# Another order of instructions, loads and PSUM banks in a fused attention and maxout-MoE kernel

## The chip, the cores and the metric

The kernel runs on one NeuronCore of a Trainium2 chip, in one launch. The metric is the device time of that core in microseconds (us). The profile of one execution gives the start and the duration of every instruction and of every DMA packet. Its engines are named as the profile names them: PE (TensorE matmul), PEld (its weight loads), ACT (ScalarE), DVE (VectorE), POOL (GpSimd) and SP (SyncE, which here only issues DMAs).

## The reference

Attention over 8 batches and 8 heads with 1152 keys of width 64; neighbouring query rows are averaged, so there are 576 queries. The result, as 4608 tokens of width 512, goes through a small MoE-like block, in which the larger of two projections is projected back.

```python
q_pool = q.reshape(B, H, S // 2, 2, D).mean(axis=3)
scores = np.matmul(q_pool, k.transpose(0, 1, 3, 2)) / np.sqrt(D)
attn = softmax(scores)
x = np.matmul(attn, v)          # then (B, H, S/2, D) -> (B*S/2, H*D) = (4608, 512)
g = np.maximum(x @ w1, x @ w2)  # w1, w2: 512 x 1024
out = g @ w_out                 # w_out: 1024 x 512
```

## The kernel before

The 64 heads are taken in 32 pairs; a pair's two heads lie in the two halves of the 128 partitions. The work of a pair goes through these steps.

- **Loads.** q, k and v of a pair, 576 KB each, come by DMAs that SP issues (`load_q` L358, `load_k` L346, `load_v` L370). The weights come in between (`w_load` L379).
- **Casts.** POOL turns them into bf16: `cast_k` L405, `cast_q` L435 (adds the two neighbouring query rows), `cast_v` L445. For the first pair small pieces are cast on ACT, POOL and DVE (`cast_k0` L418 and L424, `cast_q0` L428).
- **Transposes.** Scores need q and k with the head's width in the partitions. For pairs 0 to 4 PE transposes both (`qtrans` L533, `ktrans_pe` L552) and DVE copies the result from PSUM (L540, L568). For pairs 5 to 31 k is transposed by a DMA (`ktrans` L475, issued by SP) and q by eight DVE instructions (`qtrans_dve` L485).
- **Scores and exponentials.** Keys times queries of all pairs form one long row, which is cut into 324 groups of 512 columns for both heads. `scores` L302 (called S below) fills two PSUM banks on PE with 64-row matmuls, and `exps` L317 (E) takes the exponential on ACT. A group that crosses from an odd pair to the next is cut in two on ACT, which makes 336 instructions.
- **Values.** `av_jobs` (L621, and L636 for the last 64 queries of a pair) multiplies exponentials by values on PE with 128-row matmuls, 9 in a chunk; DVE divides by the sum (L651, L654). For some pairs POOL first copies the exponentials of the last 64 queries aside (`keep_rest` L468).
- **Transposed x.** A DMA transpose (`xtrans` L703, L712), or PE and DVE for some pairs (`xtrans_pe` L552, L730, L733, L738), brings x to xT.
- **MoE.** max(x w1, x w2) is computed as x w2 + max(x (w1 - w2), 0). POOL makes the difference of the weights (`w_diff` L506), DVE casts the rest (`w_cast` L498), PE multiplies w2 by w_out once (`w2t_job`, `w_job` L593). Then `h_jobs` (L760, 64-row matmuls) and `p_job` (L803) run over tokens; DVE or ACT empties their banks (L771/L775 and L809/L812), and SP stores the result (L829, L835). The last 256 tokens go through `z_job` (L846) and `store_z` (L866).

At the start PE also runs matmuls that nobody reads (`fill`, L515): 28 at once and 16 pairs of them, one after each letter F.

The order is written out by hand. One long string of letters is read from left to right, and each letter appends one operation to the list of its engine: S a score group, E an exponential, A a chunk of values, digits parts of the MoE jobs and the emptying of their banks, l a load, t a DMA transpose of k, x one of xT, o a store, k, q, v and d the casts and differences on POOL, r a DVE transpose, F a fill. Every engine runs its own list strictly in order, and an operation waits by semaphores for what it reads and for the buffers that it overwrites. So the string matters only by the order inside each engine, with one exception: a load also waits for an exponential, chosen by where its letter stands.

```python
K0_ENG = ('ACT', 'ACT', 'POOL', 'POOL')
PACE = 2
PACE_FROM = 40
...
        def pace():
            g = done[0] - PACE
            return [f"E{g}"] if PACE and g >= PACE_FROM else []
...
            elif c == "E":
                g, go = exp_at.pop(0)
                go()
                done[0] = g
```

`done` is the last exponential group that the string has named, so a load whose letter follows E of group 230 is issued no earlier than the end of group 228. The order of the loads stands in LOADS, the PSUM bank of each job in BANKS (one digit for each score group or job, in the order in which they are opened), the order of MoE jobs in MOE, and that of the weight casts and differences in W_CASTS and W_DIFFS. There are three buffers each for raw q, k and v and for the transposed q and k.

## Time and profile before

| | |
|---|---|
| time, median of 3 runs | 359.64 us (359.12 to 360.29) |
| the profiled execution's own time | 358.12 us |
| its span, first to last instruction | 356.4 us |
| PE busy | 346.0 us (97%) |
| ACT busy | 313.8 us (88%) |
| DVE busy | 230.1 us (65%) |
| POOL busy | 151.4 us (42%) |
| granted TensorE clock, mean | 0.999 |
| HBM read and written | 62.91 MB and 9.44 MB |

Busy time of PE is modelled at the ends of its matmuls, so overlapping matmuls read as one busy stretch. In a row of the chain of waits the columns are the start and the length in us and the work that held the end at that time. In a row of the timeline they are the start and the length in us, engine, line, operation, tiles, shape, count, and in brackets the idle time before it and what ended it. In a row of groups they are the busy us, the mean ns of one, and the idle us before. A row of stretches gives for each engine the busy us and the number of instructions, then the granted clock, the DMA engines' busy share and GB/s.

### The profile page before, as it was taken

Reading aid. Unit: us, or ns where it says so; the run is one execution under the profiler, and the core shown is the slowest. Engines: PE = TensorE matmul, PEld = TensorE weight load, DVE = VectorE, ACT = ScalarE, POOL = GpSimd, SP = SyncE. Lnnn points to the kernel's source line nnn. Section 1 sums busy time; section 2 is a strip of 40 time slices with the busy share of each in tenths; the row PEclk is TensorE's granted clock in tenths of the full one; section 3 lists DMA queues with packets and bytes.
Section 4 is the critical chain, followed back from the end, with each engine's and each line's share of the span. In section 5 each row is a group of like instructions: output and inputs, shape, how many; then the busy total and the mean of one; then the engine's idle time right before and its main releaser. Section 6 shows DMA issues by size and latency. Waiting matters only on the chain.

```text
span 356.4 us, 13757 instructions
## 1 busy us (share of the span) xinstructions
PE 346.0 (97%) x6178; PEld 218.5 (61%) x6178; DVE 230.1 (65%) x472; ACT 313.8 (88%) x354; POOL 151.4 (42%) x136
## 2 busy tenths in 40 slices
PE   7889999999899999999999999999999999999996
PEld 5556665656564675656666576556576757448753
DVE  2587589974966867985887677785586875414001
ACT  5999999999999899999999989989999796992431
POOL 2625997554564264355544455227444621010000
PEclk9999999999999999999999999999999999999999
DMA  8999999999989989998999699998999943012215
GB/s 271 403 397 398 370 255 309 280 289 261 293 252 279 315 196 350 237 301 183 278 320 260 153 230 301 237 314 234 224 299 255 267 68 75 17 32 47 61 31 148
DMA packets 76699, 84.55 MB, mean 237 GB/s; under 512 B 48480, under 2 KB 49760, under 8 KB 76640
## 3 DMA queue, kind: packets, MB, share of 16 engines
q1 hardware_dynamic: 75856, 83.15, 87.5%
q8 instruction: 48, 0.79, 0.9%
q10 hardware_dynamic: 784, 0.52, 0.5%
q14 instruction: 11, 0.09, 0.1%
HBM read 62.91 MB, written 9.44 MB: 203 GB/s over the span
## 4 chain that ended last, share of the span: by engine, by line
PE 87%; ACT 9%; DMA 2%; issue 1%; SPq 0%; DVE 0%
PE ps L803 25%; PE ps L621 20%; PE ps L302 19%; PE ps L760 16%; ACT et L317 9%; PE ps L636 3%; PE ps L593 2%; DMA qraw<-in_q_dram 2%; PE ps L846 1%; PE ps L552 0%; PE ps L533 0%; SPq L346 0%; DVE qp L428 0%; SPq L358 0%; PE ps L730 0%
## 5 line engine op out<-in xcount | busy, mean ns | idle before, releaser
L317 ACT ACTIVATE et<-ps 128x1024 bf16<-128x1024 f32 (+1 forms) x336 | 302.4, 1019 | 14.5 <-PE ps L302 9.7
L302 PE MATMUL ps<-qpT,kT 64*128 64x256 bf16 (+7 forms) x1162 | 117.3, 283 | 2.7 <-issue 1.1
L485 DVE STREAM_TRANSPOSE qpT<-qp 32x288 bf16<-32x288 bf16 x216 | 101.4, 469 | 10.4 <-PE ps L302 6.1
L760 PE MATMUL ps<-xT,wd 64*128 64x512 bf16 (+3 forms) x832 | 81.2, 311 | 0.2
L302 PEld LDWEIGHTS ps<-qpT,kT 64*128 64x128 bf16 x1162 | 48.3, 94 | 49.7 <-ACT et L317 11.3
L803 PE MATMUL ps<-wo,stage 64*128 64x512 bf16 x544 | 76.4, 376 | 0.0
L435 POOL TENSOR_TENSOR qp<-qraw 128x576 bf16<-128x576 f32 x30 | 42.1, 1406 | 61.1 <-DMA qraw<-in_q_dram 57.3
L621 PEld LDWEIGHTS ps<-vE,et 128*128 128x128 bf16 x1728 | 54.9, 97 | 13.9 <-ACT et L317 9.3
L621 PE MATMUL ps<-vE,et 128*128 128x65 bf16 x1728 | 60.7, 193 | 0.7 <-issue 0.3
L771 DVE TENSOR_SCALAR stage<-ps 128x1024 bf16<-128x1024 f32 (+3 forms) x41 | 39.7, 970 | 21.1 <-PE ps L760 20.6
L760 PEld LDWEIGHTS ps<-xT,wd 64*128 64x128 bf16 x832 | 35.6, 94 | 22.2 <-PE ps L760 1.9
L405 POOL TENSOR_SCALAR kbf<-kraw 128x1152 bf16<-128x1152 f32 x31 | 35.7, 1153 | 26.3 <-DMA kraw<-in_k_dram 25.6
L803 PE MATMUL ps<-w,xT 64*128 64x512 bf16 x272 | 40.8, 377 | 0.0
L803 PEld LDWEIGHTS ps<-wo,stage 64*128 64x128 bf16 x544 | 26.4, 94 | 20.5
L445 POOL TENSOR_SCALAR vE<-vraw 128x1152 bf16<-128x1152 f32 x24 | 27.4, 1154 | 19.4 <-PE ps L636 10.8
L809 DVE COPY stage<-ps 128x1024 f32<-128x1024 f32 x14 | 17.1, 1224 | 23.1 <-PE ps L803 23.0
L468 POOL TENSOR_SCALAR stage<-et 128x1152 bf16<-128x1152 bf16 x14 | 16.1, 1152 | 35.5 <-ACT et L317 35.5
L654 DVE TENSOR_TENSOR xnat<-ps,rc 128x256 bf16<-128x256 f32 (+2 forms) x71 | 27.6, 397 | 2.0
L651 DVE RECIPROCAL rc<-ps 128x4 f32<-128x4 f32 (+2 forms) x64 | 11.6, 182 | 25.9 <-PE ps L621 25.5
L621 PEld LDWEIGHTS ps<-stage,et 128*128 128x128 bf16 x576 | 18.1, 97 | 2.7 <-issue 2.6
L621 PE MATMUL ps<-stage,et 128*128 128x65 bf16 x576 | 19.7, 193 | 0.0
L803 PEld LDWEIGHTS ps<-w,xT 64*128 64x128 bf16 x272 | 12.5, 94 | 8.8 <-DVE stage L771 0.2
(55 smaller groups left out, 155.4 us busy)
## 6 DMA issues: line engine op xcount, KB each, us to landing
vraw<-in_v_dram SPq DMA_DIRECT2D x32, 576.0 KB, 6.1
kraw<-in_k_dram SPq DMA_DIRECT2D x31, 576.0 KB, 6.7
qraw<-in_q_dram SPq DMA_DIRECT2D x31, 576.0 KB, 6.3
out_dram<-stage SPq DMA_DIRECT2D x24, 256.0 KB, 4.1
out_dram<-stage SPq DMA_DIRECT2D x21, 128.0 KB, 3.4
xT<-in_moe_w_dram SPq DMA_DIRECT2D x4, 512.0 KB, 12.2
stage<-in_moe_w_out_dram SPq DMA_DIRECT2D x4, 512.0 KB, 14.1
stage<-in_moe_w_dram SPq DMA_DIRECT2D x4, 512.0 KB, 13.2
```

Of the source, the lines that this page charges most:

```text
L302: last = e.matmul(ps[:, h, col:col + hi - lo], kT[i % 3][rows(h), t, :], qpT[i % 3][rows(h), lo:hi], start=True, stop=True)
L317: op("ACT", lambda e: e.activation(et2[:, :, c:c + z - a], ps[:, :, a - g * W:z - g * W], EXP, scale=scale), r=[f"b{m}", f"b{m + 1}"], w=w ...
L405: op("POOL", lambda g: g.tensor_scalar(kbf[s][:, :, :, :].rearrange("p t h d -> p h t d"), kraw[r][:, :, :, :], 1.0, 1.0, ALU.mult, ALU.mu ...
L435: op("POOL", lambda g: g.tensor_tensor(qpf[s][:, :, :], qraw[r][:, :, 0, :], qraw[r][:, :, 1, :], ALU.add), r=[f"qraw{r}"], w=[f"qp{s}.0", ...
L445: return g.tensor_scalar(vE[r][:, :, :, 0:D].rearrange("p t h d -> p h t d"), vraw[s][:, :, :, :], 1.0, 1.0, ALU.mult, ALU.mult)
L485: op("DVE", lambda e: e.transpose(view[dst:dst + 32, :, 32 * pb:32 * pb + 32], qpf[s][src:src + 32, :, 32 * db:32 * db + 32]), r=[f"qp{s}. ...
L621: last = e.matmul(fb[m][:, at * 66:at * 66 + 65], et[:, a:a + P], vE[vs][:, t, half, 0:65], start=(t == 0), stop=(t == NT - 1))
L654: todo.append(evac_op("DVE", lambda e, m, z=z, at=at, num=num, dst=dst: e.tensor_tensor(dst, a(m)[z, at:at + num, 0:D], rc[k][z, at:at + n ...
L760: last = e.matmul(fb[m + k][:, 0:size], wd[z, ct, (f0 + k) * P:(f0 + k + 1) * P], xT[z, ct, n0:n1], start=(turn == 0 and ct == 0), stop=(t ...
L771: return e.tensor_scalar_max(gT[:, f0:f0 + 2, g0:g0 + size], wide[m // 2][:, :, 0:size], 0.0)
L803: last = e.matmul(fb[m + k][:, :], lhs, rhs, start=(turn == 0 and j == 0), stop=(turn == 1 and j == NC_ + NF - 1))
L809: return e.tensor_copy(osb2[:, o:o + 2, :], wide[m // 2][:, :, :])
```

## The change

No operation, shape, buffer or tile is added or removed, and no wait is added by hand: the waits follow from the order. What is written differently is the string of letters, LOADS, BANKS, MOE, W_CASTS and W_DIFFS. Only the beginnings of the long ones are shown.

```diff
-    W_CASTS = ((0, 1), (0, 3), (0, 0), (0, 2), (2, 0), (2, 1), (2, 2), (2, 3))
-    W_DIFFS = ((3, 0), (3, 1), (1, 0), (2, 0), (2, 1), (0, 0), (0, 1), (1, 1))
+    W_CASTS = ((0, 1), (0, 3), (0, 2), (0, 0), (2, 1), (2, 2), (2, 0), (2, 3))
+    W_DIFFS = ((3, 1), (3, 0), (1, 1), (0, 1), (0, 0), (2, 1), (1, 0), (2, 0))
...
-        ("k", 3), ("w", 0, 0), ("w", 0, 2), ("v", 1), ("w", 2, 0), ("w", 2, 1), ("w", 2, 2), ("q", 3),
-        ("w", 2, 3), ("w", 1, 3), ("v", 2), ("w", 1, 2), ("k", 4), ("w", 1, 1), ("q", 4), ("q", 5),
-        ("k", 5), ("v", 3), ("w", 1, 0), ("k", 6), ("q", 6), ("q", 7), ("k", 7), ("v", 4), ("v", 5),
+        ("k", 3), ("w", 0, 2), ("w", 0, 0), ("v", 1), ("w", 2, 2), ("w", 2, 1), ("w", 2, 0), ("q", 3),
+        ("w", 2, 3), ("w", 1, 3), ("v", 2), ("v", 3), ("k", 4), ("k", 5), ("q", 4), ("q", 5), ("q", 6),
+        ("w", 1, 1), ("w", 1, 0), ("w", 1, 2), ("k", 6), ("k", 7), ("q", 7), ("v", 4), ("v", 5),
...
-        "wwhhhhpphhhhpphhhhhhhhpphhhhpphhhhphhhhpphhhhphhhhphhhhpphhhhhhhhhphphh"
+        "wwhhhhpphhhhpphhhhhhhhpphhhhpphhhphhhhhpphhhhphhhhphhhphphhhhhhhphhhphh"
...
-        "0124605424023623462032424660232342630240624702402064202420472042646264246024604640164604264126402406"
+        "6424036040323373764202750042644132202646027042042604202402472046246246247024604640164604261424602406"
...
-            "luFFlulllfyKQklgfbSkKEFlgFKSgESyFFlKEFgQSbESlFkSFEFFKlEySFSgESlqFFEFQlSbEFkSQElbKvSEgSlESceAAEATcESA"
-            "EAhlkSaSEaASclEKAEglSAEcSAElvSaTaEhElTcSAESlAhAEScAElSSAcEAAlAqESa0a00aE0la0ScAE0SldQEaa00bSd0lEXSj0"
+            "lululllllylfQlfKbgKlkSglkKEFglSKlgESylSFFlEFFFFlFQElblSkFElFSlFEylFFSlKESgSqEFSQEkQbFbFESSKvESgElecA"
+            "AlEAlSAclESlAAEaTakShESAcAESEKaSgAEScSvEThEETShAESaSAcEASEcSEAAcAqEAAAaSa0lEaS0al00clEQdSl00Ea0a0Svb"
...
+            "a3a3E3r3SrSE3r333rSE7AAAElllASal0aE0St111E1S01E1e1S1E05Sv000E0S4q22E22S2E2vrSSr22ElrAqArAEArArA+AaAa"
...
```

What moves, read off the two lists of each engine:

- PE: the same matmuls. From exponential group 60 on, the lists hold the same parts of the same jobs ahead of each exponential, apart from exchanges of one to six neighbouring parts. Ahead of group 60 the order differs more: PE changes 14 times less often between kinds of job that use the array differently (64-row, 128-row, 64-column, quadrants).
- DVE: the fourth copy of the first pair's transposed k (L568, three key blocks) stands ahead of the second cast of q (L428) instead of behind it. Three emptyings of MoE banks that ACT did are done by DVE. The DVE transposes of q (L485) stand at other places, many of them later.
- SP and POOL: early loads (v3, k4, k5, q4, q5, q6) stand earlier and the last three w1 pieces later. From pair 12 on most loads stand 5 to 30 exponential groups later than before, and many casts, DMA transposes of k and xT and stores stand later too. The last line of the diff holds one such place: behind E7AAAE, the end of group 230, come three loads (l), v of pair 23 and q of pairs 24 and 25, and two letters of PE work and one of DVE later q of pair 26. Before, q of pair 24 stood behind the end of group 211.

More of the change, by code (lines that the diff above doesn't have):

```diff
@@ new lines, in bass_funnel_attn__then__act_maxout2_kernel @@
+            "EAArArEllAdSaSaEAaAadAEaXaSjXqESjjSElX2kj22Ej2rSSr2kElt2r233r3E2rtSv36E3S33E3rSv0r0E070Se0E000Sq4SEl"
+            "AAAEArSrSEAaArAaEASrSErEAqAaAaAESaSaAElxAAAlllESa1a11Er1Sr22Er22Sr1E1q1S12El52S2e2E22rSSkrE223r33Er3"
+            "e3rS2rElt22rSk22Er2Sr2tv2Er22S2E2S6333E3S3SEAAAEkSAAEllaSaAEAASa3aE3SrS3r3Eq3r333rESSr3v3Elr33r33ESk"
+            "7AAElxASSEAxvAAEASaSrElAoaAAoaEAtAaSaSaEaStXEjAAjAEAvSa0a0ElSrSe0r0ESr00rq0E0r111rE1S411E11S5SEAAAEA"
+            "Sa2aE22Ell2eSSE222k2SE6AAAEltkASaSrEArAAaEASa3a3E3rq3Sr0E0rS30r0Ell0xrS3r3E3S70l0E0xS00Er00rSSE0r0Sr"
```

54 lines of the change are left out of this document (24 added, 30 removed), and 18 rows, old and new, of the table LOADS.

## The prediction

> **What bounds the kernel now.** I read the page's busy shares first, then stretches cut where the chain of waits changes its engine, then that chain in order of time, then the timeline of the start.
>
> ```profile
> span 356.4 us, 13757 instructions
> PE 346.0 (97%) x6178; PEld 218.5 (61%) x6178; DVE 230.1 (65%) x472; ACT 313.8 (88%) x354; POOL 151.4 (42%) x136
> PE 87%; ACT 9%; DMA 2%; issue 1%; SPq 0%; DVE 0%
> ```
>
> PE holds 87% of the chain and ACT 9%. Where the 9% lies is told by the stretches:
>
> ```profile
> 0.00:10.00 10.00, 7.43 (x100) 5.49 (x100) 2.79 (x9) 5.54 (x7) 2.11 (x12) 1.00 0.83 286
> 10.00:26.00 16.00, 13.63 (x322) 8.39 (x322) 11.40 (x17) 16.00 (x20) 8.04 (x7) 1.00 1.04 398
> 26.00:45.00 19.00, 18.65 (x372) 11.74 (x371) 12.87 (x23) 18.57 (x22) 14.01 (x13) 1.00 1.00 381
> 45.00:60.00 15.00, 14.59 (x250) 8.08 (x246) 13.08 (x28) 14.99 (x18) 13.72 (x12) 1.00 1.16 283
> 60.00:180.00 120.00, 118.54 (x2165) 74.84 (x2165) 91.20 (x196) 117.70 (x133) 60.53 (x51) 1.00 1.06 273
> 180.00:320.00 140.00, 139.93 (x2410) 87.09 (x2410) 93.44 (x186) 129.69 (x145) 53.02 (x45) 1.00 0.84 203
> 320.00:356.40 36.40, 33.23 (x576) 22.86 (x572) 5.30 (x16) 11.34 (x18) 0.00 (x0) 0.99 0.30 74
> ```
>
> ```profile
> 2.24 5.91 DMA qraw<-in_q_dram
> 9.43 15.70 ACT et L317 x17
> ...
> 44.70 13.43 ACT et L317 x15
> ...
> 63.67 1.19 PE ps L621 x36
> ...
> 91.57 1.12 issue
> ...
> 119.43 2.28 PE ps L621 x72
> ```
>
> ACT has no idle time from 10 to 26 us and 0.01 us from 45 to 60 us: the exponentials set the time there. Between 26 and 45 us PE sets it, and ACT idles 0.43 us. From 60 us on PE sets it to the end: it lacks 1.46 us up to 180 us, 1.12 of them in one stall that no releaser explains ("issue"), and 0.07 us up to 320 us. What remains behind 320 us is the stores' tail. So a gain can come from the first 60 us (an earlier or denser chain of exponentials, less PE time from 26 to 45 us), or from the stall at 91.57. Behind 60 us there is little to win, and much to lose by anything that makes PE wait.
>
> **The change part by part.** Terms are made against the profiled execution, 358.12 us by its own time and 1.7 us around its span; the median of the runs, 359.64, lies 1.5 us above it.
>
> *The start.* Rows of the timeline:
>
> ```profile
> 7.91 1.03 ACT L317 ACTIVATE et<-ps 128x1024 bf16<-128x1024 f32 x1
> 8.17 0.49 DVE L428 TENSOR_TENSOR qp<-qraw 128x320 bf16<-128x320 f32 x1 [1.25 <-DMA qraw<-in_q_dram]
> 8.58 0.35 DVE L568 COPY kT<-ps 128x384 bf16<-128x384 bf16 x1
> 8.72 0.34 PE L533 MATMUL ps<-ident,qp 64*64 64x64 bf16 x10 [0.60 <-DVE qp L428]
> 9.10 0.33 DVE L540 COPY qpT<-ps 128x320 bf16<-128x320 bf16 x1 [0.17 <-PE ps L533]
> 9.43 3.77 ACT L317 ACTIVATE et<-ps 128x1024 bf16<-128x1024 f32 x4 [0.49 <-PE ps L302]
> ```
>
> The third exponential ends at 8.94 and the fourth starts at 9.43. Its scores need the last three key blocks of pair 0, copied by DVE at 8.58; that copy stands behind the cast at 8.17, which waits for a DMA that lands about then, and DVE was idle for 1.25 us ahead of it. In the changed list the copy stands ahead of the cast, so the fourth exponential can follow the third at once: 0.49 us, rounded to 0.5. The fifth needs the q part that lands at 8.15 (2.24 + 5.91). Its copy at 9.10 ends at 9.43, its scores follow some 0.4 us later, and the fifth exponential, which used to start one length (1.03) behind 9.43, can start at about 9.9. So the gain is 0.5 again, and whatever else is earlier at the start is cut off there. Ends: 0, if something else holds the fourth, and 0.6 (10.46 less the scores' end at 9.85). From there to 26 us ACT is full, so the 0.5 us is kept.
>
> *26 to 45 us.* PE sets the time, and between the exponentials 20 and 40 the new list changes kind of job 20 times instead of 24. The price of a change of kind:
>
> ```profile
> 88.26 0.72 PE L621 MATMUL ps<-stage,et 128*128 128x65 bf16 x18
> 88.91 0.60 PE L302 MATMUL ps<-qpT,kT 64*128 64x512 bf16 x4
> ```
>
> The 72 and the 36 value matmuls of the chain differ by 1.09 us (2.28 - 1.19), 0.030 us each, so 18 take 0.55; here the scores start 0.65 us behind the first of 18, and 0.10 us is the change. Four fewer are worth 0.4 us. ACT's idle time there, 0.43 us, lets it follow; that is also the upper end, and 0 the lower. The ten other changes of kind that go away lie where ACT sets the time and hides them; without that cover they would be worth 1.0 us.
>
> *From 60 us on.* PE's list has the same parts ahead of each exponential, but for exchanges of neighbours: 0. Three emptyings go from ACT to DVE: ACT idles 10 of the 140 us from 180 to 320 and DVE 47, so 0; the cover gone, about 1 us each. Fills and weight casts that change places cost 0: the fills stand in the first 26 us, in which PE has 5 us free. The last w1 pieces land later. Before the last of them the new list loads 16.3 MB; 2.9 MB come in the first 10 us (286 GB/s), the rest at 398 GB/s, so it lands at about 44 us.
>
> ```profile
> L317 ACT ACTIVATE et<-ps 128x1024 bf16<-128x1024 f32 (+3 forms) x42 | 37.7, 1045 | 1.8 <-PE ps L552 0.9 <-PE ps L302 0.8
> ```
>
> By 44.7 us (the stretch of this row) 42 exponential instructions have begun, up to group 40. POOL's last piece of that difference stands behind group 45, five groups or 5 us later: hidden, by 5 us.
>
> *Later loads and transposes.* On SP's queue the DMA transposes of k used to stand as early as their buffers allowed; now many are only 7 to 12 groups ahead of their first use (one group is 0.97 us: 140 us and 145 instructions of ACT).
>
> ```profile
> L475 SPq DMA_TRANSPOSE kT<-kbf x27: 1263/1712/3726, 43.4 to 289.0; - x27
> DMA to landing us min/median/max: 3.2/5.5/7.5
> ...
> L703 SPq DMA_TRANSPOSE xT<-xnat x24: 1188/1236/1891, 64.0 to 323.4; - x24
> DMA to landing us min/median/max: 2.5/4.4/7.1
> ...
> SPq L475 <- PE ps L302: 36.8, 17, 3.8
> ```
>
> The tightest are xT of pair 10 (behind k of pair 15, which waits for exponential 127; used at 134: 6.8 us for an issue of 0.4 and a landing of 4.4) and k of pair 21 (behind exponential 202; used by scores 212, about 8 us for 0.6 and 5.5). Both fit at the median and miss by less than 1 us at the longest landing; I take 0. Below nothing is possible too: the transposes held SP's queue for 36.8 us in all, waiting for scores to free a buffer, with loads behind them. But no PE wait on a load shows behind 60 us, so there is nothing to win.
>
> The tightest q is that of pair 24. It stands behind exponential 228, as the second of four loads:
>
> ```profile
> L317 ACT ACTIVATE et<-ps 128x1024 bf16<-128x1024 f32 (+1 forms) x239 | 214.4, 1020 | 7.2 <-PE ps L302 3.6 <-PE ps L621 2.0 <-PE ps L552 0.9
> ...
> L346 SPq DMA_DIRECT2D kraw<-in_k_dram x3: 368/368/373, 59.2 to 61.9; - x3
> ...
> DMA to landing us min/median/max: 4.3/4.9/5.8
> ...
> qraw<-in_q_dram SPq DMA_DIRECT2D x31, 576.0 KB, 6.3
> L435 POOL TENSOR_TENSOR qp<-qraw 128x576 bf16<-128x576 f32 x30 | 42.1, 1406 | 61.1 <-DMA qraw<-in_q_dram 57.3 <-DVE rc L651 3.8
> L485 DVE STREAM_TRANSPOSE qpT<-qp 32x288 bf16<-32x288 bf16 x216 | 101.4, 469 | 10.4 <-PE ps L302 6.1 <-POOL qp L435 0.8
> L651 DVE RECIPROCAL rc<-ps 128x4 f32<-128x4 f32 x48 | 8.5, 177 | 16.8 <-PE ps L621 16.4
> L654 DVE TENSOR_TENSOR xnat<-ps,rc 128x256 bf16<-128x256 f32 x57 | 24.1, 423 | 1.7
> 238.34 0.38 PE L302 MATMUL ps<-qpT,kT 64*128 64x512 bf16 x2
> ```
>
> The first row is of ACT up to 225.88 us: the 238th exponential instruction (group 228) ends there. Then 0.4 us for the issue of v (taken as the 368 ns of a k), the landing L, 1.4 for the cast, eight transposes of 0.47 and between them two reciprocals and two divisions (1.2): 225.9 + 0.4 + L + 1.4 + 3.8 + 1.2 = 232.7 + L. Scores 243, the first to need it, started at 238.34; now five more p parts of 0.22 us stand ahead of them, so PE comes there at about 239.4, and it stalls by L - 6.7 us. Three k loads issued together between 58 and 63 us landed after 4.3, 4.9 and 5.8 us, and the median of q's loads is 6.3. By these rows L is 5 to 6.3 us and the stall is 0.
>
> *The sum.* 358.12 - 0.5 - 0.4 = 357.2 us; with the 1.5 us by which the median lies higher, 358.7 us.
>
> [...] The profile's page counts the packets that carry instructions:
>
> ```profile
> q8 instruction: 48, 0.79, 0.9%
> ```
>
> PE's program comes in 48 blocks of 16 KB, and one wait of PE that nothing else explains is left in the chain, 1.12 us at 91.57. [...]
>
> **The rivals.**
>
> *A, the stall at 91.57 goes away.* For it: the two lists differ just there (scores 92 now stand ahead of exponential 91), and one block of 48 is a matter of chance. Against it: the same values burst (L621) stands ahead of it, and DMA traffic there grows by two xT transposes, a store and a k transpose. 358.7 - 1.1 = 357.6 us.
>
> *B, slower: pair 24's q lands late.* If its load shares the DMA engines with the loads of v and q issued beside it, instead of running ahead of the third, each takes 590 KB / 398 GB/s = 1.5 us of the engines, and L is 6.3 + 3.0 = 9.3 us. PE then stalls 2.6 us: 361.3 us. It decides from L = 6.7 us on, and makes the kernel slower than before by 0.3% from 8.7 us on. For it: stretches up to 180 us show the DMA engines at a share of 1.06. Against it: the three k loads landed one after another.
>
> *C, the gain of the start does not reach the end.* A further block comes late in a burst of values, 1.1 us by the row above, because transposes and stores now stand closer to those bursts: 359.8 us. The row of 48 blocks with one stall speaks against a second.
>
> **How the numbers follow.** 0.3%, 1.08 us, is about what can be told from no change; faster means under 358.56, slower over 360.72. My forecast, 358.7, has 0.35: with both terms at their upper ends it is 358.6, with both at 0 it is 359.6, and the three runs before lie up to 0.65 us off their median, which with 0.5 either way makes its own range 358.1 to 360.1: 0.14 faster, 0.21 within. A has 0.27, faster. B, with smaller misses of the same kind, has 0.25, slower. C has 0.13: 0.05 within, 0.08 slower by two such blocks or one beside a miss. Together faster 0.41, within 0.26, slower 0.33. The range goes down to A with both terms at their upper ends (357.5), that scatter of 0.5 and the 0.4 us that PE lacks elsewhere between 60 and 320 us (356.6), and up to B with 0.3 us more (361.6).
>
> **What would show it.** In the profile of the changed kernel the idle row of 0.49 us ahead of the fourth exponential is gone and the fifth starts at about 9.9 us; the chain of exponentials that begins at 44.70 begins about 0.9 us earlier; behind it the exponentials keep that lead. The issue row at 91 us tells A or C. For B, a wait of PE L302 for DVE L485 appears near 238 us. The prediction is wrong if the lead is lost between two exponentials behind 60 us, or is never there because ACT idles in the first 26 us.

## The result, and the profile after

The changed kernel is slower: 362.36 us (median of 12 runs, 360.44 to 364.67) against 359.19 us of the kernel before (12 runs beside it, 357.36 to 361.36), a ratio of 1.010 with a 95% interval of 1.0075 to 1.0125. The ratios and intervals in this document are estimated from the single runs and differ a little from the quotient of the medians (1.0088 here). Two runs that lie over 1.5% above the fastest of their kernel, one of fills_behind and one of both_moves below, are left out of the ratios. The profiled execution of the changed kernel took 361.90 us, 3.8 us more than that of before (358.12); the forecast for it was 357.2. The page of the changed kernel:

```profile
span 360.2 us, 13709 instructions
PE 347.7 (97%) x6177; PEld 220.1 (61%) x6178; DVE 231.7 (64%) x475; ACT 313.3 (87%) x351; POOL 151.1 (42%) x136
PE 70%; ACT 13%; DMA 7%; issue 4%; POOL 2%; DVE 2%; SPq 0%; POOLq 0%
```

The work is the same, but PE's share of the chain of waits fell from 87 to 70%, and ACT (9 to 13%), DMAs (2 to 7%), waits without a releaser (1 to 4%), POOL and DVE (2% each) took its place. The stretches of the changed kernel, cut as those of before (per engine busy us and instructions, then granted clock, DMA share, GB/s):

```profile
0.00:10.00 10.00, 8.64 (x96) 6.46 (x96) 2.47 (x8) 5.95 (x7) 2.98 (x12) 1.00 0.84 291
10.00:26.00 16.00, 12.65 (x302) 8.06 (x296) 10.07 (x16) 14.79 (x17) 7.18 (x6) 1.00 1.04 398
26.00:45.00 19.00, 18.25 (x370) 11.34 (x370) 12.59 (x23) 18.51 (x22) 13.24 (x12) 1.00 0.97 375
...
60.00:180.00 120.00, 117.13 (x2139) 73.63 (x2136) 85.63 (x183) 116.31 (x130) 56.29 (x47) 1.00 0.94 246
180.00:320.00 140.00, 139.44 (x2411) 87.46 (x2409) 97.59 (x198) 130.49 (x145) 60.03 (x51) 1.00 0.97 231
```

In the first 26 us ACT, which sets the time there, is busy 20.74 us instead of 21.54. From 60 to 180 us PE, which sets it there, lacks 2.87 us instead of 1.46. Which waits these are is told by the waits of PE from 60 to 320 us, first before, then changed (engine, line, what it waited for: us in total, times, longest):

```profile
PE ps L302 <- issue: 1.1, 1, 1.1
PE ps L621 <- ACT et L317: 0.3, 1, 0.3
```

```profile
PE ps L621 <- DVE xnat L654: 1.7, 1, 1.7
PE ps L621 <- ACT et L317: 0.5, 1, 0.5
PE ps L302 <- issue: 0.4, 2, 0.2
PE ps L302 <- DVE stage L809: 0.3, 1, 0.3
PE ps L760 <- DVE stage L771: 0.2, 1, 0.2
```

Three waits for DVE are new. The most useful measure is the lag: by how much the exponential of a group ends later than in the profiled execution of before. In the changed kernel, and in some of the kernels below, it is (us, from the starts and durations of ACT's instructions in the traces):

| group (its end before) | changed | cast q7 early | emptyings first | four places | before, once more |
|---|---|---|---|---|---|
| 3 (10.45) | -0.66 | -0.58 | -1.00 | -0.56 | -0.58 |
| 4 (11.37) | +0.65 | +0.71 | -0.95 | -0.56 | -0.57 |
| 20 (26.10) | +0.98 | +0.77 | -0.18 | +0.03 | -0.51 |
| 40 (45.30) | +0.97 | +0.54 | -0.18 | -0.12 | -0.66 |
| 60 (63.81) | +0.89 | +0.46 | -0.26 | -0.19 | -0.66 |
| 63 (66.56) | +2.31 | +0.46 | -0.26 | -0.19 | -0.66 |
| 160 (158.82) | +3.06 | +0.58 | -0.20 | -0.31 | -1.14 |
| 300 (296.96) | +3.36 | +0.60 | +0.12 | +0.25 | -1.06 |
| 320 (319.22) | +3.91 | +1.41 | +1.09 | +0.65 | -1.06 |

So the changed kernel loses 1.3 us between groups 3 and 4, 0.3 between 16 and 18, 1.4 between 60 and 63, 0.4 between 140 and 160, 0.43 between 300 and 304, and some tenths elsewhere. The lead of 0.5 us from the start that was forecast is there for one exponential. The last column is the unchanged kernel in a second execution (before_again below, 357.03 us): two executions of one kernel differ by up to 1.1 us.

### The profile page after: what moved, and what is told of

It is laid out like the page before. It is cut to its first block, busy times and chain, and to the rows that moved or that the text cites. A ratio compares the mean times of both kernels' runs of the same rounds, so it can differ in the third digit from the quotient of the medians.

```text
span 360.2 us, 13709 instructions
## 1 busy us (share of the span) xinstructions
PE 347.7 (97%) x6177; PEld 220.1 (61%) x6178; DVE 231.7 (64%) x475; ACT 313.3 (87%) x351; POOL 151.1 (42%) x136
## 4 chain that ended last, share of the span: by engine, by line
PE 70%; ACT 13%; DMA 7%; issue 4%; POOL 2%; DVE 2%; SPq 0%; POOLq 0%
PE ps L803 22%; PE ps L621 16%; PE ps L302 16%; ACT et L317 13%; PE ps L760 12%; DMA kraw<-in_k_dram 3%; DMA qraw<-in_q_dram 2%; PE ps L636 2%; DMA vraw<-in_v_dram 2%; PE ps L846 1%; DVE qpT L485 1%; POOL qp L435 1%; POOL kbf L405 1%; PE ps L515 1%; PE ps L593 0%
## 5 line engine op out<-in xcount | busy, mean ns | idle before, releaser
L302 PE MATMUL ps<-qpT,kT 64*128 64x256 bf16 (+7 forms) x1162 | 115.0, 285 | 1.9 <-ACT et L317 0.6
L485 DVE STREAM_TRANSPOSE qpT<-qp 32x288 bf16<-32x288 bf16 x216 | 101.4, 469 | 11.2 <-POOL qp L435 7.6
L760 PE MATMUL ps<-xT,wd 64*128 64x512 bf16 (+3 forms) x832 | 77.9, 311 | 0.5 <-DVE stage L771 0.2
L302 PEld LDWEIGHTS ps<-qpT,kT 64*128 64x128 bf16 x1162 | 47.5, 94 | 49.4 <-ACT et L317 12.6
L803 PE MATMUL ps<-wo,stage 64*128 64x512 bf16 x544 | 73.8, 376 | 0.0
L771 DVE TENSOR_SCALAR stage<-ps 128x1024 bf16<-128x1024 f32 (+3 forms) x43 | 40.3, 943 | 30.5 <-PE ps L760 30.2
L803 PE MATMUL ps<-w,xT 64*128 64x512 bf16 x272 | 38.1, 376 | 0.0
L809 DVE COPY stage<-ps 128x1024 f32<-128x1024 f32 x15 | 18.4, 1225 | 22.8 <-PE ps L803 22.6
L468 POOL TENSOR_SCALAR stage<-et 128x1152 bf16<-128x1152 bf16 x14 | 16.1, 1153 | 16.3 <-ACT et L317 16.2
```

What stands on the lines that cost most here:

```text
L302: last = e.matmul(ps[:, h, col:col + hi - lo], kT[i % 3][rows(h), t, :], qpT[i % 3][rows(h), lo:hi], start=True, stop=True)
L485: op("DVE", lambda e: e.transpose(view[dst:dst + 32, :, 32 * pb:32 * pb + 32], qpf[s][src:src + 32, :, 32 * db:32 * db + 32]), r=[f"qp{s}. ...
L760: last = e.matmul(fb[m + k][:, 0:size], wd[z, ct, (f0 + k) * P:(f0 + k + 1) * P], xT[z, ct, n0:n1], start=(turn == 0 and ct == 0), stop=(t ...
L771: return e.tensor_scalar_max(gT[:, f0:f0 + 2, g0:g0 + size], wide[m // 2][:, :, 0:size], 0.0)
L803: last = e.matmul(fb[m + k][:, :], lhs, rhs, start=(turn == 0 and j == 0), stop=(turn == 1 and j == NC_ + NF - 1))
L809: return e.tensor_copy(osb2[:, o:o + 2, :], wide[m // 2][:, :, :])
```

## The experiments

The edits are given as the order of operations on one engine: ck, cq, cv are the casts of k, q, v (with the pair), rem the copy of the last 64 queries' exponentials (L468), f a pair of fills (L515), f0 the 28 fills ahead of all, q.0.4 the transposes of q's second part of pair 0 (L533), S a score group, qt a transposition of q on DVE (L485), ev.h and ev.p the emptyings of MoE banks (L771, L809). What an edit does not show stays as in the kernel that it starts from. Ratios are to the kernel before in the same series.

### Fills, the cast of q7, both, and earlier loads

The timeline of the changed kernel at its start, PE's rows and ACT's:

```profile
7.51 0.61 PE L302 MATMUL ps<-qpT,kT 64*128 64x256 bf16 x4
8.06 1.67 PE L515 MATMUL ps<-rem 128*128 128x128 bf16 x14
9.66 0.47 PE L533 MATMUL ps<-ident,qp 64*64 64x64 bf16 x10
...
10.99 2.87 ACT L317 ACTIVATE et<-ps 128x1024 bf16<-128x1024 f32 x3 [1.20 <-PE ps L302]
```

The cast that q.0.4 needs ended at 7.85, but PE came to it at 9.66, behind 14 fill matmuls, and the fifth exponential waited 1.20 us. And the chain of waits around the wait of 1.7 us:

```profile
54.55 6.31 DMA vraw<-in_v_dram
60.86 0.07 issue
60.94 1.16 POOL vE L445
62.09 1.11 POOL rem L468
63.21 1.38 POOL qp L435
64.59 0.02 issue
64.61 0.47 DVE qpT L485
...
65.66 0.44 DVE xnat L654
66.10 0.14 issue
66.23 1.25 PE ps L621 x36
```

The load of v5 lands late. POOL's cast of q7, whose data had landed at 55.5, stands behind the cast of v5; DVE's transposes of q7, needed only from about 74 us on, wait for that cast; the division of pair 4's values stands behind them on DVE; and PE needs its bank. Four edits of the changed kernel:

```diff
  PE, kernel "fills_behind"
  S.3
- f.1 f.2 f.3 f.4 f.5 f.6 f.7
  q.0.4
+ f.1 f.2
  S.4
+ (the other five pairs behind S.4 to S.6)
...
  POOL, kernel "cast_q7_early"
  ck.7
+ cq.7
  cv.4
  cv.5
  rem.4
- cq.7
  cq.8
...
  kernel "both_moves": the two together
...
  kernel "loads_earlier"
- PACE = 2
+ PACE = 4
```

> The changed kernel with the seven fills that stand between the scores of group 3 and the transposes of q's second part (q.0.4) moved behind those transposes and behind groups 4 to 6; nothing else moves. Theory: in the changed kernel PE works off 14 fill matmuls (1.60 us of the chain at 8.12) while the cast that the transposes need is ready at 7.85, so the fifth exponential waits 1.20 us; with the fills behind, it starts at about 9.8 instead of 10.99, ACT stays full, and the end comes 1.2 us earlier: 362.4 - 1.2 = 361.2 us. Rival: the start does not reach the end, because PE and the loads set the time between 20 and 65 us (PE waits 1.69 us at 64.54 for a load that comes when it comes): the fifth exponential is as early, but the lead is gone by group 63 and the time is 362.4 us.

> The changed kernel with POOL's cast of q of pair 7 ahead of the casts of v of pairs 4 and 5 and of the copy of pair 4's exponentials, as far forward as behind the cast of k of pair 7; nothing else moves. Theory: on DVE the transposes of q7 (L485) stand ahead of the division of pair 4's values (L651, L654); they wait for the cast of q7, which stands on POOL behind the cast of v5, whose load lands only at 60.86. So a late v5 holds PE for 1.69 us at 64.54. With the cast of q7 at 55.5 us that wait is gone and the end comes 1.4 us earlier (the lag of the exponentials there grows by 1.42 us): 361.0 us. Rival: the lateness is that of the load of v5 itself, and PE meets it next at the values of pair 5 or at the transposes of q8: a wait of the same size behind 62 us, gain under 0.4 us, 362.0 to 362.4 us.

> Both moves together: fills behind the transposes of q, and the cast of q7 ahead of those of v4 and v5. Theory: the two add up, 362.4 - 1.2 - 1.4 = 359.8 us, that is within 0.3% of the kernel before (359.2). Rival (the start is absorbed before 65 us): only the second counts, 361.0 us. Rival (late load met again): only the first, 361.2 us.

> The changed kernel with each paced load two exponential groups (about 1.9 us) earlier: PACE 4 instead of 2. Theory: the wait at 64.5 comes from the late landing of v5 by way of the queues of POOL and DVE; v5 is issued at 52.7 instead of 54.55, lands at about 59.0, the transposes of q7 are through 1.8 us earlier and the wait of 1.69 us goes; the smaller ones of the same kind at 146.6 (q15 lands at 143.65, 0.17 us of PE) and 301.0 (0.26 us) go too: 362.4 - 1.4 - 0.6 = 360.4 us. Rival: the DMA engines are full there (share 0.97 to 0.99), so that a load issued earlier lands no earlier, or takes the place of another that is needed first: 362.4 us or more. Second rival: only the order in the queues counts, not the time of the loads: 362.4 us with the wait at 64.5 unchanged.

| kernel | median us (runs) | ratio, 95% interval |
|---|---|---|
| fills_behind | 361.96 (6) | 1.0098 (1.0067 to 1.0130) |
| cast_q7_early | 360.46 (12) | 1.0070 (1.0049 to 1.0091) |
| both_moves | 360.06 (12) | 1.0055 (1.0031 to 1.0079) |
| loads_earlier | 361.19 (6) | 1.0092 (1.0064 to 1.0120) |

The cast of q7 does what the theory says where it stands. POOL's rows in cast_q7_early, the casts of q7 and of v5:

```profile
55.99 1.40 POOL L435 TENSOR_TENSOR qp<-qraw 128x576 bf16<-128x576 f32 x1 [0.27 <-DMA qraw<-in_q_dram]
...
60.70 1.15 POOL L445 TENSOR_SCALAR vE<-vraw 128x1152 bf16<-128x1152 f32 x1 [2.09 <-DMA vraw<-in_v_dram]
```

v5 is cast as late as in the changed kernel, yet PE has no wait between 58 and 70 us and the lag does not grow between groups 60 and 63. The kernels below repeat this: in all seven profiled executions with this move the lag grows there by 0.03 us at most, and in the four that keep the changed order of loads and casts there (changed, fills_behind, early_fills, cast_q30_alone) by 0.66 to 1.42. So a late v5 is harmless once nothing that PE needs soon stands behind it in the queues; the rival of a late load that PE meets next falls. In time the intervals of 1.010 and 1.0070 still overlap; of the 1.4 us expected 1.1 show (0.3% of 359). The mean ratio of the seven series, some with further edits, is 1.0048, that of the four 1.0092: 0.44%, or 1.6 us. With the fills behind, the fifth exponential starts 1.3 us earlier in the profiled execution (lag at group 4 -0.69, at group 20 0.01), but the median does not move: 1.2 us were expected, 0.1 measured. So both_moves (1.0055) stands where the second move alone was expected (361.0 against 359.2, 1.005) and not at the sum of both. Earlier loads take the wait at 64.5 us away too (none in the profiled execution), so the late load is a cause beside the order, but the median falls by 0.3 us where 2.0 were expected: in that execution PE waits 1.6 us at 206 us for nothing that the profile shows.

That the start's gain did not come out raised a doubt about its cause. In loads_earlier, whose lists are those of the changed kernel up to 40 us, the wait of 1.20 us ahead of the fifth exponential is missing too, with all seven pairs of fills in place.

### Old loads under the new order, and the first step alone

The first two kernels have the changed kernel's lists of PE, ACT and DVE, and the lists of SP and POOL of before (LOADS and W_DIFFS too); the second has its fills spread in addition. The third is the kernel before with the first step of the prediction alone.

```diff
  DVE, kernel "copy_first" (from the kernel before)
+ copy of the last three key blocks of pair 0 (L568)
  second cast of q (L428)
- copy of the last three key blocks of pair 0 (L568)
  PE
  S.2
+ their transposes (L552)
  f.4 f.5
- their transposes (L552)
  f.6
+ S.3
  q.0.4
- S.3
```

> The changed kernel's lists of PE, ACT and DVE with the lists of SP and POOL (loads, DMA transposes, stores, casts, and the exponential behind which each load stands) of the kernel before. Theory: from 60 us on the changed kernel loses by late loads and casts alone, by way of transposes of q on DVE that wait for them with emptyings behind; with the old loads the waits of PE at 64.5, 146.6 and 301.0 are gone and only the start stays (lag 0.65 us at group 4, 0.98 at group 20): 1.0 us above the kernel before, a ratio of 1.003. Rival: the new order of PE and DVE is slower by itself, whatever the loads: the waits stay and the ratio is that of the cast of q7 moved (1.007) or of the changed kernel (1.010).

> The same (PE, ACT, DVE of the changed kernel, SP and POOL of the kernel before) with the fills of the start behind the transposes of q's second part, spread so that no more than one pair of them stands between two score groups up to group 5. Theory: both losses are undone, and what is left is the start that the prediction spoke of: the fourth and fifth exponential 0.5 to 0.7 us earlier than in the kernel before, of which 0 to 0.5 us reach the end: ratio 0.9985 to 1.000. Rival: the lead is lost before group 20 for another reason, and the ratio is that of the old loads alone, 1.003.

> The kernel before with its start alone changed as the first step of the prediction has it: the transposes (PE) and the copy (DVE) of the last three key blocks of pair 0 ahead of the second cast of q, and the scores of group 3 ahead of the transposes of q's second part. Theory: the wait of 0.49 us ahead of the fourth exponential goes, the fifth starts at about 9.9 instead of 10.35, the lead of 0.45 us is kept to the end: 0.45 us less, ratio 0.9987. Rival: between 20 and 45 us ACT waits for PE anyway (0.4 us), and the lead is gone by group 40: ratio 1.000.

The ratios are 1.0097 (1.0062 to 1.0132), 1.0128 (1.0091 to 1.0165) and 1.0008 (0.9983 to 1.0033). The old loads take the three waits away (lag 0.68 at groups 60 and 63), but others come: the profiled chain of old_loads at 82 to 90 us reads

```profile
82.67 4.28 issue
...
86.99 1.42 POOL qp L435
88.41 0.02 issue
88.43 0.47 DVE qpT L485
88.90 1.12 DVE stage L809
90.02 0.05 issue
90.06 0.39 PE ps L302 x4
```

It is the same pattern at another place: POOL waits 4.3 us for the load of a q (the row "issue" at 82.67; POOL's own waits name the DMA), so that the cast is late; DVE's transposes wait for the cast, an emptying stands behind them, and PE waits 1.7 us for the bank. So DVE's and POOL's lists have to fit each other, and this mixture of two plans fits less. The expectation for old_loads (1.003) misses; its rival's 1.010 is met in number but not for its reason, that the same waits stay. start2_old_loads misses both its values (0.9985 to 1.000, and 1.003).

The first step alone gains 0.41 us at group 4, and the profiled execution keeps it to group 280 (-0.72); in the median it can't be told from nothing. What the step was to win is itself not a property of the kernel before: in its second execution the second cast of q starts at 6.87 instead of 8.17, because the DMA landed earlier, and the fourth exponential waits for nothing.

### Emptyings ahead of waiting transposes, and more fills at the front

```diff
  DVE, kernel "emptyings_first" (with the cast of q7 moved as above)
- qt.15 (first)
  ev.h.3.2
+ qt.15 (first)
...
- qt.30 (last two)
  ev.p.12
+ qt.30 (last two)
...
  POOL, kernel "three_places": that, and
+ cq.30
  ck.30
- cq.30
...
  PE, kernel "early_fills" (from the changed kernel)
  f0
+ f f
  q.0.0
...
  S.3
- f f
  f f f f f
  q.0.4
...
  kernel "four_places": "three_places" with the fills of "early_fills"
...
  PE, kernel "late_fills_before" (from the kernel before)
  f0
- f f
  k.0.0
...
  S.4
+ f f
```

> The changed kernel with the cast of q7 moved forward and, in DVE's list, two emptyings of MoE banks ahead of transposes of q that wait for late casts: that of tokens' block 3, part 2 (L771) ahead of the first transpose of q15, and that of output pair 12 (L809) ahead of the last two transposes of q30. No load, cast or PE instruction moves beside the cast of q7. Theory: the price of the late loads is only what stands behind the waiting transpose in DVE's queue: with the emptyings ahead of it the waits of PE at 146.6 (0.17 to 0.82 us) and 301.0 (0.26 to 0.93 us) go, 0.8 us (the lag of the exponentials grows by 0.37 and 0.45 there) below the cast of q7 alone, ratio 1.0045. Rival: PE needs the late q itself next: ratio 1.007.

> The changed kernel with the cast of q7 moved forward, the two emptyings ahead of waiting transposes of q15 and q30, and POOL's cast of q30 (whose data lies ready from about 270 us) ahead of the cast of k30, which waits for a load that lands at 290.7 to 293.5. Theory: what was left at 298 us in the kernel with the emptyings first, 0.69 us of PE waiting for the transposes of q30 themselves, goes with the cast: 0.7 us below that kernel, ratio 1.0005. Rival: PE waits there for k30 next (its DMA transpose lands at 297.9, used at 298.5): ratio 1.002 as with the emptyings alone.

> The changed kernel with two of the seven pairs of fills that stand behind the scores of group 3 moved to where the kernel before has two pairs: behind the first 28, ahead of the first transposes; nothing else moves. Theory: at the start PE has two rates (fills 107 or 56 ns apart, scores of 256 columns 185 or 117 ns). In the profiled executions with 32 fills at the front (the kernel before, and it with the copy first) PE turns to the fast rate between 4.3 and 5.9 us; with 28 it turned fast at about 5.2 us in three of eight, and stayed slow to about 10.5 us or longer in five, the changed kernel among them. What costs is not the fills' place ahead of the transposes but the slow rate, which the shorter burst at the front allows. With 32 fills PE is fast by 6 us, the fifth exponential starts at about 10.0 instead of 10.99, and group 20 ends at about 26.1 instead of 27.07: 0.5 to 1.0 us less, a ratio to the kernel before of 1.007 to 1.0085. Rival: the fills in front of the transposes of q's second part cost as such (five pairs are still there), and the rate is chance: no change, 1.010.

> The same with two pairs of fills moved to the front. Theory: both losses of the changed kernel, start and late casts, are undone: 0.5 to 1.0 us less than without the fills, ratio 0.998 to 0.9995. Rival: the start does not reach the end (the values of pair 1 wait for the load of v1, which lands at 23.6 us, in every execution with a fast start): ratio as without the fills, 1.0005.

> The kernel before with its two pairs of fills at the front moved behind the scores of group 4, so that 28 fills stand at the front as in the changed kernel; nothing else moves. Theory: PE stays at the slow rate to about 10 us in about two of three executions; the transposes and scores of groups 0 to 4 take 0.1 to 0.2 us longer each, the fourth and fifth exponential come up to 1 us later, and that reaches the end: 0.3 to 1.0 us more, ratio 1.001 to 1.003. Rival: the front needs no more than 28 fills, and two pairs fewer ahead of the first transposes only let them start 0.1 to 0.3 us earlier: ratio 0.999 to 1.000.

The results differed from one another by more than the edits explained, so four more were run: one cast alone, the kernel with three places a second time, the fills with the emptyings, and one more execution of the kernel before.

> The changed kernel with nothing but POOL's cast of q30 moved ahead of the cast of k30. It tells why the kernel with three places mended stands at 1.009 while the one without this move stands at 1.002. If the move itself costs 2 us, this kernel stands at 1.016. If it is worth the 0.3 to 0.9 us of PE's wait at 301 us and the rest is chance of the start and the clock, it stands at 1.0075 to 1.010.

> The kernel with three places mended, unchanged, loaded anew. If its 1.009 comes from its list, it comes again; if it comes from the start (PE slow to about 10 us in five of the nine profiled executions with 28 fills at the front) and from the halved clock (granted clock 0.995 and below in 6 of 12 runs of the changed kernel, in 0 to 2 of 23 to 28 of the kernel before), this one may stand anywhere from 1.001 to 1.009, and its runs with a mean granted clock below 0.998 are the slower ones.

> The kernel with the cast of q7 and the two emptyings moved (1.0024), with two pairs of fills at the front as well, without the move of the cast of q30. If 32 fills at the front make the start fast each time, PE is fast by 6 us in its profile and the ratio is 0.999 to 1.001; if the rate at the start is chance with 32 fills too, it is 1.002.

> The kernel before once more, one look: a further start with 32 fills at the front. If these make PE fast, its scores of group 1 take 117 ns each by 6.6 us; if the rate is chance, they take 185 ns in about half of such looks.

| kernel | fills at the front | median us (runs) | ratio, 95% interval | PE fast by |
|---|---|---|---|---|
| changed | 28 | 362.36 (12) | 1.0100 (1.0075 to 1.0125) | 10.6 us |
| early_fills | 32 | 361.05 (12) | 1.0059 (1.0035 to 1.0083) | 4.1 us |
| cast_q30_alone | 28 | 362.59 (10) | 1.0111 (1.0077 to 1.0145) | 5.4 us |
| emptyings_first | 28 | 359.12 (12) | 1.0024 (0.9996 to 1.0051) | 5.3 us |
| fills_and_emptyings | 32 | 359.31 (12) | 1.0023 (0.9994 to 1.0053) | 3.9 us |
| three_places | 28 | 361.68 (6) | 1.0094 (1.0063 to 1.0126) | 5.3 us |
| three_again | 28 | 361.17 (12) | 1.0062 (1.0033 to 1.0090) | 10.8 us |
| four_places | 32 | 358.87 (12) | 1.0008 (0.9985 to 1.0032) | 5.7 us |
| late_fills_before | 28 | 358.71 (12) | 0.9993 (0.9970 to 1.0016) | 3.9 us |

"PE fast by" is read from the profiled execution alone: the first time at which scores of 256 columns follow each other after 117 ns instead of 185, or fills after 56 ns instead of 107.

Of these only three_places lies clearly away from both values that were expected for it (1.0005 and 1.002). The intervals of the others hold at least one expected value and mostly more, so their medians decide little between theory and rival. fills_and_emptyings had a fast start in its profiled execution, yet 1.0023 where 0.999 to 1.001 was expected with one; late_fills_before and four_places lie nearest to their rivals (0.999 to 1.000, and 1.0005).

**DVE's queue.** The cast of q7 with the two emptyings moved (and no load) takes 0.76% off, from 1.0100 to 1.0024; with 32 fills it takes off 0.36% (1.0059 to 1.0023). In the traces the emptying moved at q15 is worth its wait: between groups 145 and 149 the lag grows by 0.31 us in the changed kernel and by 0.00 in all five executions with the emptying moved. At q30 it is worth nothing by itself. What stands at 298 us in emptyings_first is a wait for the transposes of q30 themselves, the last two of which now stand behind the emptying:

```profile
296.20 1.23 DVE L809 COPY stage<-ps 128x1024 f32<-128x1024 f32 x1
...
298.46 0.39 PE L302 MATMUL ps<-qpT,kT 64*128 64x384 bf16 x4 [0.69 <-DVE qpT L485]
```

There the rival was right: DVE was free to empty, but PE needed q30 next, whose cast stood on POOL behind that of k30, whose load landed at 290.7. The lag grows there by 0.86 us between groups 300 and 304 (0.43 in the changed kernel). With the cast of q30 ahead it grows by 0.05 us in cast_q30_alone and by 0.3 us in the three executions with the emptying moved too. In the medians that move does not show: with it the ratio is 0.1% higher, 0.5% higher and 0.15% lower in the three pairs that differ by it (mean of the two series with three places: 1.0078). Nor do the traces have the 0.46%, 1.6 us, by which emptyings_first lies below cast_q7_early. So a difference of half a percent between two of these kernels can't be put down to one edit.

**All of them.** With the four edits PE's waits from 60 to 320 us are

```profile
PE ps L760 <- issue: 0.2, 1, 0.2
PE ps L621 <- POOL vE L445: 0.2, 1, 0.2
PE ps L621 <- ACT et L317: 0.2, 1, 0.2
```

and the time is that of the kernel before (1.0008), as far as can be told; with two edits less, emptyings_first (1.0024) can't be told from it either. No version beat it by a measurable amount.

**The start.** The kernel with the emptyings first has the lists of the changed kernel on every engine up to 50 us. Its rows of the same work:

```profile
7.31 0.96 PE L515 MATMUL ps<-rem 128*128 128x128 bf16 x14
8.19 0.34 PE L533 MATMUL ps<-ident,qp 64*64 64x64 bf16 x10
...
5.68 7.49 ACT L317 ACTIVATE et<-ps 128x1024 bf16<-128x1024 f32 x8 [0.83 <-PE ps L552]
```

The same 14 fills take 0.96 us instead of 1.67, the transposes 0.34 instead of 0.47, and ACT runs through. So the place of the fills costs only where PE works them off slowly; in fills_behind PE was slow too, and with the fills behind the transposes nothing was lost at group 4 (lag -0.69). In the traces fills follow each other after 107 ns in all first microseconds and after 56 ns later. With 28 fills at the front the change came only at about 10.5 us or later in six of the twelve profiled executions (the changed kernel, fills_behind, both_moves, cast_q7_early, three_again and start2_old_loads), and by 3.9 to 5.4 us in the others; with 32 it came by 6.3 us in all six. By chance, at one in two, six of six would come in one case of 64. In time 32 fills take off 0.41% (1.0100 to 1.0059), 0.01% (1.0024 to 1.0023) and 0.70% (1.0078 to 1.0008), 0.37% in the mean; but the kernel before loses nothing with 28, against the expectation of 0.1 to 0.3%, and its one profiled start was fast.

The traces hold one more thing that bears on it, their record of the granted clock. It begins where PE turns fast: at 4.20 us in the kernel before, where the distance of the fills goes from 107 to 55 ns, and at 10.16 in the changed kernel, between fills 106 ns apart up to 9.3 us and scores 117 ns apart from 10.56 on. All stretches between its entries are whole multiples of 3.41 us (6.83, 20.48 and 351.57 us among them; only the last is cut off by the end). In the six slow starts it begins at 10.03 to 13.38 us, in the eleven other executions with such a record (late_fills_before has none) at 3.84 to 6.01 us. All six with 32 fills are among these eleven, and the changed kernel and emptyings_first, whose lists are the same there, are on different sides. No trace shows steps ahead of the first entry. Counted back in steps of 3.41 us as if they ran there too (an estimate), the six slow starts had one at 3.1 to 3.6 us, when PE had worked for 2.0 to 2.5 us, and one at 6.5 to 7.0 us, and turned fast at neither; and no execution shows what 32 fills do when a step lies as early as 3.6 us. That the list's shorter front makes slow starts more frequent is possible and not shown.

**The clock.** The granted clock of each run tells of a second loss. One step of 3.41 us at a clock of 0.50 lowers the mean of 360 us to 0.995 (1.7 of 360 us; the profiled run of old_loads, at 0.50 from 24.45 to 27.85 us, has a mean of 0.995). Of 136 runs of kernels with the changed order on PE, 50 had a mean clock of 0.995 or less; of 101 runs of the kernel before, 8. Stretches of early_fills, whose profiled execution was one of them:

```profile
21.05:24.45 3.40, 1.96 (x60) 1.08 (x52) 2.20 (x4) 2.75 (x4) 0.63 (x1) 1.00 1.04 387
24.45:27.85 3.40, 2.89 (x59) 1.79 (x52) 3.03 (x6) 3.09 (x5) 0.53 (x1) 0.51 1.05 397
27.85:31.30 3.45, 3.45 (x56) 2.77 (x54) 2.61 (x5) 3.31 (x4) 1.30 (x1) 0.50 1.04 397
```

The clock is halved for 6.8 us, behind 3.4 us in which PE was busy 1.96, and the lag grows by 1.7 us between groups 20 and 40 (from -0.11 to +1.63). In the kernel before, the same place reads

```profile
21.00:24.40 3.40, 2.73 (x70) 1.75 (x70) 3.37 (x5) 3.40 (x5) 0.74 (x1) 1.00 1.04 386
```

What makes PE idle there in the changed order is a wait without a releaser in the middle of 18 transposes of k of pair 3, here in the changed kernel's chain of waits:

```profile
22.61 0.26 PE ps L552 x17
22.87 0.85 issue
23.72 0.19 PE ps L552
```

It stands there for 0.8 to 1.4 us in 13 of the 14 profiled executions with the changed order on PE (the exception is cast_q7_early), and in none of the four with that of before or a slight variant of it; late_fills_before has one of 0.62 us at 22.35, in values. In all 13 PE goes on 1.2 to 1.5 us after a packet of 16 KB on the instruction queue has landed (at 22.46 in the changed kernel); that it waits for this packet is an estimate, and no run shows it. Within nine kernels that had at least three runs on either side of that clock, the runs with the lower clock are 0.9 us longer in the mean (0.05 to 1.8). At 37% against 8% of the runs that makes 0.3 us of the difference of 3.6 us (1.0% of 359).

## Why the prediction was wrong, point by point

**The start, forecast -0.5, measured +0.65 at group 4 and +0.98 at group 20.** The copy ahead of the cast did its work: the wait of 0.49 us ahead of the fourth exponential is gone (lag -0.66 at group 3). The next exponential gave it back, by the step "Fills and weight casts that change places cost 0: the fills stand in the first 26 us, in which PE has 5 us free". The list's 14 fills ahead of q.0.4 cost nothing when PE is fast (lag -0.95 in emptyings_first) and 1.3 us when it is slow, as it was in the profiled execution of the changed kernel; how many of its runs start slowly is not known. PE's free time was counted over the stretch, not at the place where the fills stand. The step "From there to 26 us ACT is full, so the 0.5 us is kept" fails as well, also after a fast start: the wait at 22.87 us (21.3 to 23.1 us in the other executions) takes 0.25 to 0.75 us between groups 16 and 20 (emptyings_first from -0.89 to -0.18, four_places from -0.55 to +0.03) in all 13 executions that have it. cast_q7_early, which lacks it, loses nothing there, and the kernel before with the copy moved keeps its lead of 0.41. No step of the prediction had a wait of PE at that place. And the 0.5 us was read from one execution: the second one of the same kernel does not have that wait.

**26 to 45 us, forecast -0.4, measured 0.0.** From the end of group 20 to that of group 40, before and changed:

```profile
26.10:45.30 19.20, 18.85 (x374) 11.74 (x366) 13.03 (x25) 18.77 (x22) 14.31 (x13) 1.00 1.06 379
```

```profile
27.07:46.28 19.21, 18.62 (x370) 11.62 (x364) 12.95 (x24) 18.72 (x23) 14.52 (x13) 1.00 1.01 358
```

PE's busy time fell by 0.23 us, about half of what four changes of kind were to be worth. ACT idles as long as before (0.49 us against 0.43), and the 20 groups take as long. The saved time became idle time of PE: the upper bound (ACT's idle time) had been taken as room that PE's work would fill, while the two waits of ACT hang on single bursts.

**Behind 60 us, forecast 0, measured +2.8** (from 0.98 us to the 3.8 us by which the profiled executions differ; the differences of 1.5, 0.4 and 2.8 make the 4.7 us between forecast and profiled execution)**.** The step that failed is that of the later loads and transposes: "Both fit at the median and miss by less than 1 us at the longest landing; I take 0." For each late transfer it asked when its own consumer needs it. It did not ask what stands behind a waiting instruction on its engine. q7 came in time for its own scores, but its transposes held a division (1.4 us); those of q15 and q30 held an emptying each (0.31 and 0.43 us of lag). These three are 2.2 of the 2.8 us; the rest is spread over tenths. A landing beyond 6.7 us, from which rival B priced pair 24, came at pair 15 with 8.0 us:

```profile
135.63 8.02 DMA qraw<-in_q_dram
...
143.72 1.42 POOL qp L435
```

and at pair 24 itself the load took 6.8 us, and PE waited 0.2 us there (without a releaser). k of pair 21, which was to miss by less than 1 us at the longest landing, held PE in four of the twelve profiled executions with the changed list of loads: 0.2, 0.3, 0.83 (both_moves) and 0.97 us (fills_and_emptyings). So the size of that margin was right, though taking it as 0 was not; the queues behind the late transfers, which cost more, were left out.

**The rivals.** A (the stall at 91.57 us goes) is a matter of the execution more than of the list: it takes 0.64 us in the second execution of the kernel before, 0.65 in both_moves, 0.51 in loads_earlier and nothing in four_places. In the changed kernel 0.2 us of it are left at 94 us, and a wait of 0.55 us for ACT at 95.3 takes the gain back. B was the right kind (a late q) with the wrong pairs and price. C, that the gain of the start does not reach the end, is what happened between groups 16 and 20 in the executions with a fast start, but not for C's reason and not in a burst of values: the wait without a releaser lies in transposes of k, at 22.87 us, and that a late block causes it is not shown.

**The row of 48 blocks.** The row is the same in the changed kernel (48 packets, 0.79 MB). It does not say whose instructions they are; that they are PE's is an estimate from the counts (PE's matmuls and weight loads are 12,356 of the 13,757 instructions before). Most of these packets land without such a wait of PE: between 60 and 320 us the kernel before has one without a releaser, of 1.1 us, and the changed kernel two, of 0.2 us each. But the wait at 22.9 us takes 0.8 to 1.4 us in nearly every execution with the changed order, and the one at 91 us up to 1.1. So the 1.1 us that A and C reckon with are of the right size, and one place more has such a wait than the chain before shows; that late blocks make these waits, as C has it, no run shows.

## What to carry to other kernels

When a transfer or a cast is moved later, look at the whole queue of the engine that waits for it: price what stands behind the waiting instruction, above all the emptying of a bank that another engine needs, and put work that can be late last. Matmuls that nobody reads are part of the plan: what they cost depends on the rate that PE happens to have where they stand (0.96 or 1.67 us for the same 14), and a gap in PE's work can be followed by some microseconds at half the clock (6.8 us at 0.50 in early_fills, behind a wait of 1.4 us). A term of half a microsecond read from one execution is smaller than what two executions of one kernel differ by, and wants a second profile.

## What was not expected of the hardware

- PE has two rates at the start that the column of the granted clock does not show: it reads 1.00 from the first microsecond in the changed kernel, while fills follow each other after 107 ns up to 9.3 us and after 56 ns from 10.95 us on; the trace's record of the clock begins at 10.16 us. In the changed kernel a front of 3.2 us of fills (1.12 to 4.29 us) with gaps of 0.24 us at most behind it up to 10 us did not turn PE fast; with 28 fills at the front PE turned fast at about 10.5 us or later in six of the twelve profiled executions and by 3.9 to 5.4 us in the others. What decides it no run shows.
- The clock falls to 0.50 for 3.4 us or twice that in mid-kernel after a step of 3.4 us in which PE was busy only 45 to 58% (1.54 us in old_loads, 1.78 in start2_old_loads, 1.96 in early_fills). The busy time alone does not decide it: in the steps that end at 195.13 us in old_loads and at 68.19 us in the changed kernel PE was busy 1.79 and 1.96 us, and the clock stayed at 1.00. What does decide it no run shows.
- Behind the longest waits without a releaser PE goes on about 1.3 us after a packet of the instruction queue has landed: 1.26 us after 22.46 in the changed kernel, 1.29 after 91.40 in the kernel before, 1.27 after 206.48 in loads_earlier.
- A kernel of which all engines' lists are fixed still varies by 3 to 4 us from run to run (358.0 to 361.9 in four_places). Which of these events an execution meets is part of that; how much, no run here shows.
